# First pair's row maxima in another order, with fills, bias rows and loads moved

## The chip, the cores and the metric

The kernel runs on one core of one Trainium2 chip. The time is device microseconds of a whole execution, and the number compared is the median of several runs. Profiles are of one execution each. The engines are TensorE (PE, its weight loads apart as PEld), VectorE (DVE), ScalarE (ACT), GpSimd (POOL) and SyncE (SP), which here only issues DMAs.

## The reference

Three stages follow one another: attention with queries averaged over pairs of positions, a mixture of 8 experts in which each token goes to one expert, and a dense layer of width 2048 with x * tanh(softplus(x)). The change lies in the attention alone:

```python
q_pool = q.reshape(B, H, S // 2, 2, D).mean(axis=3)      # B 2, H 8, S 1152, D 64
scores = scale * np.matmul(q_pool, k.transpose(0, 1, 3, 2))
scores = scores - np.max(scores, axis=-1, keepdims=True)
attn = np.exp(scores)
attn = attn / (np.sum(attn, axis=-1, keepdims=True) + 1e-09)
attn_out = np.matmul(attn, v)
```

So each of the 576 pooled queries of a head needs the maximum over 1152 keys before its exponentials can be taken.

## The kernel before

The 16 heads are worked on as 8 pairs (p from 0 to 7; h is the head within a pair). A pair has 9 steps (t from 0 to 8), one for each 128 keys. A step makes the scores of its keys for both heads (`scores`, L322 and L324), takes their exponentials on ScalarE into a tile "pt", and every third step multiplies three such tiles by the values (`pv`, L341) and sums them (`psums`, L373). Operands are split in a high part in TensorE's own format (fp32r) and a low rest: `qhi` (tile "qs") and `khi` (tile "at", in halves c of 576 keys) are ScalarE copies, `qlo` (the lower 64 partitions of "qs") and `klo` (tile "Bt") are subtractions on VectorE or GpSimd. `qsum` adds the two positions of each pooled query (tile "tq"), `qcopy` copies the high half of the queries to "qb". Rows 64 and 65 of "Bt" are ones (`bias_rows`), and rows 64 and 65 of "qb" hold the negative maximum and its rounding rest; so the product at L322 adds the low part and subtracts the maximum at once.

The maxima are made before a pair's steps begin, in 9 units: 4 blocks of 128 queries for each head and one shared last unit with the last 64 queries of both heads (`qmix` puts them together in "QM"). A unit has three products of 128x384, called thirds, made by `max_chunk` (L237, and L241 for the shared unit): third 0 takes the first 384 keys and is reduced by VectorE (L103); third 1 takes the difference of the second and the last 384 keys (`kdiff`, tile "kx") and goes through a relu on ScalarE; third 2 takes the last 384 keys, and one fused VectorE operation (L251) adds the relu and takes the maximum. Third 0 of pair 0 uses the three "mx" banks of the PSUM, thirds 1 and 2 of pair 0 the three "sc" banks; for later pairs all use "mx".

`max_cols` then makes columns with the negative maximum and its rest in "Mt" (a reduction, a scaling, and the last operation L97). `max_rows` turns them into rows with TensorE transposes (L295 for queries 0 to 511, L297 for the last 64) and copies the rows into "qb" on ScalarE: 512 and 64 columns for each head. All heads' rows of the first 512 lie in one bank.

For pairs 1 to 7 the units are spread over the steps of earlier pairs (`step_chunks`). For pair 0 there is no earlier step: its 27 thirds are issued ahead of step 0, in the order that `ahead` gives (third 1 of the next unit, third 2 of this one, third 0 of the next), and the other work of this lead stage is put between them by a table, `sched`, filled with `at_step`; steps with p = -1 are the lead. `sched` also gives the order by hand for steps 0 to 8 of pair 0: slot 0 comes right after the scores, slot 1 after the step's first units, slots 4, 2 and 3 behind the value products. Each engine works strictly in the order written; waits follow from the data. `warm` issues junk products of 128x512 on TensorE (L721) whose result nobody reads: 13 at the start, then 9, 7 and 3 around `max_rows`. Tokens (`G.tensor_copy(wait_, ...)`) make GpSimd wait for one element before it goes on.

Buffers that matter: "kd" (raw keys) 3, so that the fourth load, pair 1's second head, waits until `klo` and `khi` of the first keys are done; "pt" 4, shared by raw queries of pairs 0 and 1 and the exponentials; "tq" 3; "kx" 3. All loads named here are issued by SyncE in the order written; the second halves of later queries are added by DMAs that GpSimd issues (`add_q`).

Of the kernel before, what the change touches and what calls it, by code (L numbers as in the profile page):

```python
# [9 lines left out]
F32 = mybir.dt.float32  # L10
# [5 lines left out]
ALU = mybir.AluOpType  # L16
# [4 lines left out]
P = 128  # L21
B, H, S, D = 2, 8, 1152, 64
SQ = S // 2
# [61 lines left out]
def kernel(ctx, tc, cst, qt, kt, v, wgo, w1, w2, wio, out):  # L85
# [4 lines left out]
    def act(out, in_, func=AF.Copy, **kw):  # L90
        A.activation(out=out, in_=in_, func=func, **kw)  # L91

    def tt(eng, out, a, b, op):
        eng.tensor_tensor(out=out, in0=a, in1=b, op=op)  # L94
# [100 lines left out]
    def qlo(p, h):  # L195
        q_ = QS[p, h][64:]
        tt(G if p > 1 or (p, h) == (0, 1) else V, q_, tqt[p, h][64:], q_.bitcast(F32), ALU.subtract)

# [3 lines left out]
    def qb_(p, h):  # L202
        if (p, h) not in QB:
            QB[p, h] = ap.tile([P, SQ], F32R, name="qb", bufs=NBL)
        return QB[p, h]
# [46 lines left out]

    def ahead(units):
        n = len(units)
        seq_ = [(units[0], 0), (units[0], 1)]
        for i in range(n):
            if i + 1 < n:
                seq_ += [(units[i + 1], 1)]
            seq_ += [(units[i], 2)]
            if i + 1 < n:  # L260
                seq_ += [(units[i + 1], 0)]
        return [(*u, c) for u, c in seq_]

    units = [(h, j) for h in range(2) for j in range(4)] + [(0, 4)]
    chunks = ahead(units)
    FIRST = [[0, 1], [2], [3], [4, 5], [6, 7], [8], []]

# [23 lines left out]
    def max_rows(p):  # L291
        mt = Mt[p % 2]
        ps0 = mxp.tile([P, 512], F32, name="mx")
        for j in range(4):
            T.transpose(ps0[:34, j * P:(j + 1) * P], mt[:, j, :], ident)  # L295
        ps1 = mxp.tile([P, 512], F32, name="mx")
        T.transpose(ps1[:34, :P], mt[:, 4, :], ident)  # L297
        for h in range(2):
            act(qb_(p, h)[64:66, :512], ps0[32 * h:32 * h + 2, :])
            act(qb_(p, h)[64:66, 512:], ps1[:2, 64 * h:64 * h + 64])  # L300
# [257 lines left out]
    def at_step(p, t, *fns, slot=0):  # L558
        sched.setdefault((9 * p + t, slot), []).extend(fns)

    at_step(-1, 1, lambda: None, lambda: None, lambda: qhi(0, 1), lambda: (khi(0, 1, 0), qlo(0, 1)))
    at_step(-1, 2, lambda: None, lambda: None, lambda: khi(0, 1, 1), lambda: (klo(0, 0, 0), klo(0, 0, 1)))
    at_step(-1, 3, lambda: qmix(0, 1), lambda: (klo(0, 1, 0), klo(0, 1, 1)))
    at_step(-1, 4, lambda: (qcopy(0, 0), load_k(1, 1), load_q(1, 1)))
    at_step(-1, 5, lambda: qcopy(0, 1))
    at_step(-1, 6, lambda: (qsum(1, 0), khi(1, 0, 0), kdiff(1, 0)))
    at_step(-1, 7, lambda: (qhi(1, 0), khi(1, 0, 1)))
    at_step(-1, 8, lambda: (max_cols(0), qlo(1, 0)))
    at_step(0, 0, lambda: (qmix(1, 0), klo(1, 0, 0), klo(1, 0, 1), kdiff(1, 1), load_q(2, 0), load_k(2, 0)))
    at_step(0, 0, lambda: qsum(1, 1), slot=3)  # L570
    at_step(0, 1, lambda: (qhi(1, 1), khi(1, 1, 0), qlo(1, 1), add_q(2, 0)), slot=1)
    at_step(0, 2, lambda: khi(1, 1, 1))
    at_step(0, 3, lambda: qmix(1, 1), slot=1)
    at_step(0, 2, lambda: (klo(1, 1, 0), klo(1, 1, 1), load_q(2, 1), load_k(2, 1)), slot=1)
    at_step(0, 3, lambda: (qhi(2, 0), kdiff(2, 0), qlo(2, 0), add_q(2, 1)), slot=2)
# [4 lines left out]
    at_step(5, 1, lambda: G.memset(sm[:, :64], 0.0), slot=3)  # L580
    at_step(-1, 8, lambda: load_v(0))
    wait_ = ap.tile([P, 1], F32, name="wait")
# [76 lines left out]
    for i in range(2):  # L659
        G.memset(Mt[i], 0.0)  # L660
        G.memset(Mp[i], 0.0)
    G.memset(one16, 1.0)
    G.memset(zero16, 0.0)
# [9 lines left out]
    def bias_rows(i):  # L673
        act(Bt[i][64:66, :].rearrange("p (a b) -> p a b", b=P), one16[64:66].unsqueeze(1).to_broadcast([2, KT, P]))

    for i in range(2):
        bias_rows(i)
    for i in range(2, NBL):
        at_step(0, i, lambda i=i: bias_rows(i))
    qsum(0, 0)  # L680
# [5 lines left out]
    load_k(1, 0)  # L686
    SP.dma_start(out=wbd, in_=wgo)
    khi(0, 0, 0)
    qlo(0, 0)
    qmix(0, 0)  # L690
    khi(0, 0, 1)
    G.tensor_copy(wait_[64:], QS[0, 0][64:, SQ - 1:].bitcast(F32))
    kdiff(0, 0)
    qsum(0, 1)
# [22 lines left out]
    def warm(n):  # L717

        w = scp.tile([P, 512], F32, name="sc").rearrange("p (a b) -> p a b", b=P)
        for _ in range(n):  # L720
            mm(w, lhsT=one16, rhs=one16.unsqueeze(1).to_broadcast([P, 4, P]), start=True, stop=True)  # L721

    warm(13)
    for g in range(-9, 0):
        tasks = list(sched.get((g, 0), ()))
        for i in range(4):
            if tasks:
                tasks.pop(0)()
            if chunks:
                max_chunk(0, *chunks.pop(0))  # L730
        for f in tasks:
            f()
        if g == -1:
            assert not chunks
            warm(9)
            max_rows(0)
            warm(7)
            for u in FIRST[0]:
                max_chunk(1, *units[u], 1)
            warm(3)  # L740

# [894 lines left out]
```

## Time and profile before

| | |
|---|---|
| median of 3 runs | 651.24 us (649.33 to 652.01) |
| the profiled execution | 648.99 us, its span 647.1 us, mean granted TensorE clock 0.989 |
| PE busy | 618.0 us, 96% of the span |
| DVE busy | 486.1 us, 75% |
| ACT busy | 396.4 us, 61% |
| POOL busy | 254.5 us, 39% |
| chain that ended last | PE 66%, DVE 15%, ACT 7%, issue 5%, DMA 3%, POOL 2% |

The span begins with the first instruction; what lies around it in the execution's time is 1.9 us. Busy shares are means over stages that have different limits; the change touches about the first 35 us, and the rows below are mostly from there. In a timeline a row is one instruction or a run of like ones: its start, its duration, engine, line, operation, tiles and count, and in brackets how long the engine had been idle before it and what released it.

### The profile page before, as it was taken

The numbers are of one execution on the slowest core, as the hardware profiler recorded it, in microseconds if no ns is written. First come the engines' busy times: TensorE is split into PE (matmuls) and PEld (weight loads), VectorE is DVE, ScalarE is ACT, GpSimd is POOL, SyncE is SP. The second block draws the span as 40 slices with busy tenths as digits, with TensorE's granted clock in tenths as the row PEclk, the third lists the DMA queues.
The fourth block names the chain that finished last, engine by engine and source line by source line (L and its number), as shares of the span: only waits on it lengthen the run. The fifth ranks groups of instructions, "written<-read, shape, count | busy, mean of one in ns | idle before, by whom it ended". The sixth has DMA issues, their size and how long they took to land.

```text
span 647.1 us, 11371 instructions
## 1 busy us (share of the span) xinstructions
PE 618.0 (96%) x4144; PEld 496.3 (77%) x4144; DVE 486.1 (75%) x995; ACT 396.4 (61%) x841; POOL 254.5 (39%) x235
## 2 busy tenths in 40 slices
PE   7999999999999999589999999999999999999996
PEld 4667778787787776279868868697879999999993
DVE  4667797978787879558847778249998778878775
ACT  7789888887887675244555367346655545454453
POOL 6747638384664342242215035103223332323221
PEclk8999999999999999699999999999999999999999
DMA  6956655364451332498798496820000200000001
GB/s 248 322 152 207 174 179 125 109 189 147 120 191 34 123 86 66 132 325 305 247 389 316 172 351 238 318 81 0 2 0 1 95 5 1 2 32 18 1 0 52
DMA packets 27405, 89.86 MB, mean 139 GB/s; under 512 B 2886, under 2 KB 7631, under 8 KB 23250
## 3 DMA queue, kind: packets, MB, share of 16 engines
q1 hardware_dynamic: 22176, 74.80, 32.6%
q0 software_dynamic: 3568, 8.79, 5.9%
q10 hardware_dynamic: 1602, 5.51, 2.6%
q8 instruction: 34, 0.56, 0.4%
q14 instruction: 25, 0.20, 0.1%
HBM read 79.65 MB, written 9.97 MB: 138 GB/s over the span
## 4 chain that ended last, share of the span: by engine, by line
PE 66%; DVE 15%; ACT 7%; issue 5%; DMA 3%; POOL 2%; SPq 0%; ACTq 0%; DVEq 0%; POOLq 0%
PE pv L341 10%; PE ops L1454 8%; PE mx L237 5%; PE sc L324 5%; PE sc L322 5%; DVE l L97 4%; DVE n L97 3%; DMA wt<-in_w 3%; PE zps L1023 3%; PE pv L373 3%; PE zps L1024 3%; PE zps L1025 3%; PE yp L1023 3%; PE yp L1025 2%; PE yp L1024 2%
## 5 line engine op out<-in xcount | busy, mean ns | idle before, releaser
L100 POOL TENSOR_SCALAR u<-u 128x384 f32<-128x384 f32 x46 | 58.2, 1265 | 147.0 <-ACT u L91 147.0
L91 ACT ACTIVATE pt<-sc 128x320 f32<-128x320 f32 (+1 forms) x198 | 87.8, 490 | 10.7 <-PE sc L322 7.9
L341 PE MATMUL pv<-pt,vt 128*64 128x288 f32 x576 | 75.6, 411 | 0.0
L91 ACT ACTIVATE l<-n,two 128x384 f32<-128x384 f32 x48 | 29.6, 617 | 74.6 <-DVE n L97 74.6
L103 DVE TENSOR_REDUCE Mp<-mx 128x1 f32<-128x384 f32 x72 | 40.1, 556 | 39.6 <-PE mx L237 34.6
L324 PE MATMUL sc<-qs,at 128*128 128x320 f32 (+1 forms) x264 | 67.4, 299 | 0.0
L322 PE MATMUL sc<-qb,Bt 66*128 66x320 f32 (+1 forms) x264 | 66.6, 296 | 0.0
L1023 PE MATMUL zps<-yh,wh 128*128 128x384 f32 x184 | 63.0, 343 | 1.8 <-DVE n L97 1.8
L1025 PE MATMUL zps<-yl,wh 128*128 128x384 f32 x184 | 61.9, 337 | 0.0
L341 PEld LDWEIGHTS pv<-pt,vt 128*64 128x64 f32 x576 | 39.0, 137 | 28.5 <-issue 5.2
L1024 PE MATMUL zps<-yh,wd 128*128 128x384 f32 x176 | 59.1, 336 | 0.0
L1454 PE MATMUL ops<-wh,gl 128*128 128x512 f32 x144 | 56.9, 400 | 1.4 <-DVE gl L94 0.8
L1454 PE MATMUL ops<-wh,gh 128*128 128x512 f32 x144 | 57.2, 397 | 0.9 <-ACT gh L91 0.9
L1454 PE MATMUL ops<-wd,gh 128*128 128x512 f32 x135 | 53.2, 394 | 0.0
L100 POOL TENSOR_SCALAR dm<-dm 128x512 f32<-128x512 f32 x21 | 41.5, 1977 | 23.1 <-ACT dm L91 23.0
L94 POOL TENSOR_TENSOR Bt<-kd,at 64x576 fp32r<-64x576 f32 x32 | 45.7, 1442 | 4.2 <-ACT at L91 4.1
L324 PEld LDWEIGHTS sc<-qs,at 128*128 128x128 f32 x264 | 46.2, 189 | 1.1 <-issue 0.8
L97 DVE SCALAR_TENSOR_TENSOR l<-n,r 128x384 f32<-128x384 f32 x48 | 26.7, 556 | 25.6 <-ACT r L91 25.6
L322 PEld LDWEIGHTS sc<-qb,Bt 66*128 66x128 f32 x264 | 45.3, 189 | 0.0
L1023 PEld LDWEIGHTS zps<-yh,wh 128*128 128x128 f32 x184 | 34.6, 188 | 4.6 <-DVE n L97 3.1
L237 PE MATMUL mx<-at,qs 128*128 128x384 f32 x120 | 35.7, 363 | 2.3 <-DVE qs L94 0.8
L1053 POOL DMA_INDIRECT ybuf<-y,six x11 | 11.2, 1020 | 66.2 <-ACT y L91 48.4
(327 smaller groups left out, 1615.0 us busy)
## 6 DMA issues: line engine op xcount, KB each, us to landing
wt<-in_w SPq DMA_DIRECT2D x32, 1024.0 KB, 8.0
kd<-in_kt SPq DMA_DIRECT2D x16, 576.0 KB, 5.3
wraw<-in_wio SPq DMA_DIRECT2D x11, 512.0 KB, 4.6
wd<-in_wio SPq DMA_DIRECT2D x11, 512.0 KB, 4.1
vt<-in_v SPq DMA_DIRECT2D x8, 576.0 KB, 5.7
wraw<-in_wio ACTq DMA_DIRECT2D x7, 512.0 KB, 5.8
tq<-in_qt SPq DMA_DIRECT2D x12, 288.0 KB, 4.4
tq<-in_qt POOLq DMA_DIRECT2D x12, 288.0 KB, 6.0
```

What stands on the lines that cost most here:

```text
L91: A.activation(out=out, in_=in_, func=func, **kw)
L94: eng.tensor_tensor(out=out, in0=a, in1=b, op=op)
L97: V.scalar_tensor_tensor(out=out, in0=a, scalar=s, in1=b, op0=op0, op1=op1)
L100: eng.tensor_scalar(out=out, in0=a, scalar1=s1, scalar2=s2, op0=op0, op1=op1)
L237: mm(ps, lhsT=QS[p, h][:, j * P:(j + 1) * P], rhs=keys(h), start=True, stop=True)
L322: mm(o, lhsT=Bt[(2 * p + h) % NBL][:66, ks], rhs=QB[p, h][:66, qs_], start=False, stop=last_, skip_group_check=not (first and last_))
L324: mm(o, lhsT=At[p, h][:, ks], rhs=QS[p, h][:, qs_], start=first, stop=False, skip_group_check=not (first and last_))
L341: mm(pvt[p][f][64 * h:64 * h + 64, :HQ], lhsT=vt[p][:, t, h, :], rhs=Pt[p, t][:, h, f * HQ:(f + 1) * HQ], start=t == 0, stop=t == KT - 1, ...
L1023: mm(out_, lhsT=a, rhs=c, start=first, stop=False)
L1024: mm(out_, lhsT=b_, rhs=c, start=False, stop=False)
L1025: mm(out_, lhsT=a, rhs=d, start=False, stop=last_)
L1454: mm(opt[b_, j], lhsT=(g_, g_, gl_)[i], rhs=(wo, wl_, wo)[i], start=f == 0 and i == 0, stop=f == NF - 1 and i == 2)
```

## The change

`qlo` of pair 0's second head is made in two pieces, queries 0 to 255 and 256 to 575. The order of pair 0's thirds is written out anew (`order0`): third 0 of units 0 and 1 first, then third 1 of both, and from there on third 0 of a unit, its third 1 and third 2 of the unit before it; around units 3 to 5 third 2 comes earlier. The fills of the lead hang on named thirds (`tasks`) instead of `sched`. After each third 2 stands one junk product; further junk products are 4, 2 and 1 instead of 9, 7 and 3, and they write a bank of the value products ("pv0") instead of an "sc" bank. The first `kdiff` goes to VectorE, and GpSimd's token waits for it. Of pair 0's second key halves `klo` moves behind the maxima, into step 0; pair 1's `klo` moves from step 0 to step 2, its second head's to step 3, and GpSimd waits there for the second head's `qlo`, and before step 0's work for the columns "Mt". `qmix` of pair 1's first head moves from step 0 to step 3; `qcopy` of pair 0 and `khi` of pair 1 come behind the last third 1. All four `bias_rows` are made at the start, the last two on VectorE. The raw queries of pair 1's second head and the values of pair 0 are loaded in the first burst; the keys of pair 1's second head are loaded after `max_rows`. For pair 0 `max_rows` transposes the second head's columns once more into a bank of their own, and VectorE copies the row from there.

```diff
--- before.py
+++ after.py
@@ -193,8 +193,9 @@
         act(QS[p, h], tqt[p, h])
 
     def qlo(p, h):
-        q_ = QS[p, h][64:]
-        tt(G if p > 1 or (p, h) == (0, 1) else V, q_, tqt[p, h][64:], q_.bitcast(F32), ALU.subtract)
+        for c in (slice(0, 256), slice(256, SQ)) if (p, h) == (0, 1) else (slice(0, SQ),):
+            q_ = QS[p, h][64:, c]
+            tt(G if p > 1 or (p, h) == (0, 1) else V, q_, tqt[p, h][64:, c], q_.bitcast(F32), ALU.subtract)
 
     def qmix(p, h):
         act(QM[p % 2][:, 192 * h:192 * h + 64], QS[p, h][:, 4 * P:].bitcast(F32))
@@ -250,19 +251,11 @@
             r_ = rlt.pop((p, h, j))
             V.tensor_tensor_reduce(out=r_, in0=ps, in1=r_, scale=1.0, scalar=-3.0e38, op0=ALU.add, op1=ALU.max, accum_out=Mp[p % 2][:, h, j, 1:2])
 
-    def ahead(units):
-        n = len(units)
-        seq_ = [(units[0], 0), (units[0], 1)]
-        for i in range(n):
-            if i + 1 < n:
-                seq_ += [(units[i + 1], 1)]
-            seq_ += [(units[i], 2)]
-            if i + 1 < n:
-                seq_ += [(units[i + 1], 0)]
-        return [(*u, c) for u, c in seq_]
-
     units = [(h, j) for h in range(2) for j in range(4)] + [(0, 4)]
-    chunks = ahead(units)
+    order0 = [(0, 0), (1, 0), (0, 1), (1, 1), (0, 2)]
+    for i in range(2, 9):
+        order0 += [(i, 0), (i, 1)] + [(u, 2) for u in ({3: (2, 3), 4: ()}.get(i, (i - 1,)))]
+    order0 += [(8, 2)]
     FIRST = [[0, 1], [2], [3], [4, 5], [6, 7], [8], []]
 
     def step_chunks(p, t):
@@ -295,8 +288,14 @@
             T.transpose(ps0[:34, j * P:(j + 1) * P], mt[:, j, :], ident)
         ps1 = mxp.tile([P, 512], F32, name="mx")
         T.transpose(ps1[:34, :P], mt[:, 4, :], ident)
+        pa = [(act, ps0[32 * h:32 * h + 2, :]) for h in range(2)]
+        if p == 0:
+            ps2 = mxp.tile([P, 512], F32, name="mx")
+            for j in range(4):
+                T.transpose(ps2[:2, j * P:(j + 1) * P], mt[:, j, 32:34], ident)
+            pa[1] = V.tensor_copy, ps2[:2, :]
         for h in range(2):
-            act(qb_(p, h)[64:66, :512], ps0[32 * h:32 * h + 2, :])
+            pa[h][0](qb_(p, h)[64:66, :512], pa[h][1])
             act(qb_(p, h)[64:66, 512:], ps1[:2, 64 * h:64 * h + 64])
 
     F0 = 256
@@ -558,27 +557,19 @@
     def at_step(p, t, *fns, slot=0):
         sched.setdefault((9 * p + t, slot), []).extend(fns)
 
-    at_step(-1, 1, lambda: None, lambda: None, lambda: qhi(0, 1), lambda: (khi(0, 1, 0), qlo(0, 1)))
-    at_step(-1, 2, lambda: None, lambda: None, lambda: khi(0, 1, 1), lambda: (klo(0, 0, 0), klo(0, 0, 1)))
-    at_step(-1, 3, lambda: qmix(0, 1), lambda: (klo(0, 1, 0), klo(0, 1, 1)))
-    at_step(-1, 4, lambda: (qcopy(0, 0), load_k(1, 1), load_q(1, 1)))
-    at_step(-1, 5, lambda: qcopy(0, 1))
-    at_step(-1, 6, lambda: (qsum(1, 0), khi(1, 0, 0), kdiff(1, 0)))
-    at_step(-1, 7, lambda: (qhi(1, 0), khi(1, 0, 1)))
-    at_step(-1, 8, lambda: (max_cols(0), qlo(1, 0)))
-    at_step(0, 0, lambda: (qmix(1, 0), klo(1, 0, 0), klo(1, 0, 1), kdiff(1, 1), load_q(2, 0), load_k(2, 0)))
+    at_step(0, 0, lambda: (klo(0, 0, 1), klo(0, 1, 1), kdiff(1, 1), load_q(2, 0), load_k(2, 0)))
     at_step(0, 0, lambda: qsum(1, 1), slot=3)
     at_step(0, 1, lambda: (qhi(1, 1), khi(1, 1, 0), qlo(1, 1), add_q(2, 0)), slot=1)
     at_step(0, 2, lambda: khi(1, 1, 1))
-    at_step(0, 3, lambda: qmix(1, 1), slot=1)
-    at_step(0, 2, lambda: (klo(1, 1, 0), klo(1, 1, 1), load_q(2, 1), load_k(2, 1)), slot=1)
+    at_step(0, 3, lambda: (qmix(1, 0), qmix(1, 1)), slot=1)
+    at_step(0, 2, lambda: (G.tensor_copy(wait_[64:], QS[1, 1][64:, :1].bitcast(F32)), klo(1, 0, 0), klo(1, 0, 1), load_q(2, 1)), slot=1)
+    at_step(0, 3, lambda: (klo(1, 1, 0), klo(1, 1, 1), load_k(2, 1)), slot=1)
     at_step(0, 3, lambda: (qhi(2, 0), kdiff(2, 0), qlo(2, 0), add_q(2, 1)), slot=2)
     at_step(0, 4, lambda: (qcopy(1, 0), qcopy(1, 1), load_q(3, 0), load_q(3, 1)), slot=1)
     at_step(0, 6, lambda: (khi(2, 0, 0), khi(2, 0, 1), qhi(2, 1), add_q(3, 0), add_q(3, 1)), slot=1)
     at_step(0, 6, lambda: (after(2, 0), qlo(2, 1), kdiff(2, 1)), slot=3)
     at_step(0, 8, lambda: (G.tensor_copy(tri, cc("tri")), G.tensor_copy(iota16, iota), G.tensor_copy(code16, cc("code")), G.tensor_copy(tid16, cc("tid"))), slot=1)
     at_step(5, 1, lambda: G.memset(sm[:, :64], 0.0), slot=3)
-    at_step(-1, 8, lambda: load_v(0))
     wait_ = ap.tile([P, 1], F32, name="wait")
 
     def after(n, u):
@@ -659,7 +650,7 @@
     for i in range(2):
         G.memset(Mt[i], 0.0)
         G.memset(Mp[i], 0.0)
-    G.memset(one16, 1.0)
+    V.memset(one16, 1.0)
     G.memset(zero16, 0.0)
     G.memset(xu4, 0.0)
     G.memset(sm, 0.0)
@@ -671,12 +662,11 @@
         G.memset(e2[:, h, h:h + 1], 1.0)
 
     def bias_rows(i):
-        act(Bt[i][64:66, :].rearrange("p (a b) -> p a b", b=P), one16[64:66].unsqueeze(1).to_broadcast([2, KT, P]))
-
-    for i in range(2):
+        cp_ = act if i < 2 else V.tensor_copy
+        cp_(Bt[i][64:66, :].rearrange("p (a b) -> p a b", b=P), one16[64:66].unsqueeze(1).to_broadcast([2, KT, P]))
+
+    for i in range(NBL):
         bias_rows(i)
-    for i in range(2, NBL):
-        at_step(0, i, lambda i=i: bias_rows(i))
     qsum(0, 0)
     qhi(0, 0)
     load_q(0, 1)
@@ -685,12 +675,13 @@
     load_q(1, 0)
     load_k(1, 0)
     SP.dma_start(out=wbd, in_=wgo)
+    load_q(1, 1)
+    load_v(0)
     khi(0, 0, 0)
     qlo(0, 0)
-    qmix(0, 0)
     khi(0, 0, 1)
-    G.tensor_copy(wait_[64:], QS[0, 0][64:, SQ - 1:].bitcast(F32))
-    kdiff(0, 0)
+    kdiff(0, 0, V)
+    G.tensor_copy(wait_, KD[0, 0][:, :1].bitcast(F32))
     qsum(0, 1)
     kdiff(0, 1)
 
@@ -716,28 +707,35 @@
 
     def warm(n):
 
-        w = scp.tile([P, 512], F32, name="sc").rearrange("p (a b) -> p a b", b=P)
+        w = pvp.tile([P, 512], F32, name="pv0").rearrange("p (a b) -> p a b", b=P)
         for _ in range(n):
             mm(w, lhsT=one16, rhs=one16.unsqueeze(1).to_broadcast([P, 4, P]), start=True, stop=True)
 
     warm(13)
-    for g in range(-9, 0):
-        tasks = list(sched.get((g, 0), ()))
-        for i in range(4):
-            if tasks:
-                tasks.pop(0)()
-            if chunks:
-                max_chunk(0, *chunks.pop(0))
-        for f in tasks:
-            f()
-        if g == -1:
-            assert not chunks
-            warm(9)
-            max_rows(0)
-            warm(7)
-            for u in FIRST[0]:
-                max_chunk(1, *units[u], 1)
-            warm(3)
+    tasks = {
+        (1, 1): lambda: (qhi(0, 1), qlo(0, 1), klo(0, 0, 0)),
+        (2, 1): lambda: (khi(0, 1, 0), klo(0, 1, 0), qsum(1, 0), kdiff(1, 0)),
+        (3, 1): lambda: khi(0, 1, 1),
+        (4, 1): lambda: qmix(0, 0),
+        (5, 1): lambda: (qmix(0, 1), khi(1, 0, 0)),
+        (8, 1): lambda: (qhi(1, 0), qcopy(0, 0), qcopy(0, 1), khi(1, 0, 1)),
+    }
+    for i, c in order0:
+        max_chunk(0, *units[i], c)
+        if (i, c) in tasks:
+            tasks[i, c]()
+        if c == 2:
+            warm(1)
+    warm(4)
+    max_cols(0)
+    qlo(1, 0)
+    G.tensor_copy(wait_, Mt[0][:, 0, 1:2])
+    max_rows(0)
+    load_k(1, 1)
+    warm(2)
+    for u in FIRST[0]:
+        max_chunk(1, *units[u], 1)
+    warm(1)
 
     def run(g, slot):
         for f in sched.get((g, slot), ()):
```

## Rows read from the trace of the kernel before

**Rows 1.** Busy time by stage: stretch, each engine's busy us (instructions), PEclk, DMA share, GB/s.

```profile
7.00:23.27 16.27, 13.82 (x57) 8.41 (x57) 10.53 (x31) 11.44 (x26) 15.26 (x13) 0.90 0.73 280
23.27:34.01 10.74, 9.06 (x50) 7.04 (x49) 6.95 (x18) 9.20 (x21) 6.56 (x6) 1.00 0.79 257
...
60.00:100.00 40.00, 39.84 (x341) 30.93 (x340) 33.02 (x75) 33.65 (x79) 22.48 (x22) 1.00 0.56 168
```

**Rows 2.** Timeline, VectorE, 4 to 20 us; the last row is from 44.86.

```profile
4.59 0.76 DVE L94 TENSOR_TENSOR tq<-pt 128x576 f32<-128x576 f32 x1 [4.59 <-DMA pt<-in_qt]
...
7.52 0.56 DVE L103 TENSOR_REDUCE Mp<-mx 128x1 f32<-128x384 f32 x1 [0.67 <-PE mx L237]
...
9.71 0.56 DVE L251 CUSTOM_DVE_ANT_0 wd<-sc,wd 128x384 f32<-128x384 f32 x1 [1.63 <-PE sc L237]
...
10.66 0.55 DVE L251 CUSTOM_DVE_ANT_0 wd<-sc,wd 128x384 f32<-128x384 f32 x1
...
13.56 0.56 DVE L251 CUSTOM_DVE_ANT_0 wd<-sc,wd 128x384 f32<-128x384 f32 x1 [0.93 <-PE sc L237]
...
18.75 0.08 DVE L251 DVE_READ_ACCUMULATOR2_ANT Mp<- 128x1 f32 x1
...
19.28 0.61 DVE L97 SCALAR_TENSOR_TENSOR Mt<-mfin,Mt 128x10 f32<-128x10 f32 x1
...
44.86 0.18 DVE L97 SCALAR_TENSOR_TENSOR Mt<-mfin,Mt 128x10 f32<-128x10 f32 x1
```

**Rows 3.** Timeline, GpSimd, 7 to 20 us.

```profile
7.01 0.18 POOL L692 COPY wait<-qs 64x1 f32<-64x1 f32 x1 [4.09 <-DVE qs L94]
...
7.28 0.99 POOL L94 TENSOR_TENSOR kx<-kd 128x384 fp32r<-128x384 f32 x1
...
8.23 1.42 POOL L94 TENSOR_TENSOR tq<-pt 128x576 f32<-128x576 f32 x1
...
12.93 4.20 POOL L94 TENSOR_TENSOR Bt<-kd,at 64x576 fp32r<-64x576 f32 x3
...
18.44 1.41 POOL L94 TENSOR_TENSOR tq<-pt 128x576 f32<-128x576 f32 x1
```

**Rows 4.** Timeline, ScalarE and TensorE, 19 to 24 us.

```profile
19.89 0.68 ACT L91 ACTIVATE qs<-tq 128x576 fp32r<-128x576 f32 x1 [2.11 <-POOL tq L94]
...
19.94 0.61 PE L295 MATMUL mx<-cs,Mt 128*34 128x128 f32 x4
...
20.50 1.67 PE L721 MATMUL sc<-one 128*128 128x512 f16 x7
...
21.16 1.52 ACT L91 ACTIVATE qb<-mx 2x512 fp32r<-2x512 f32 x4
...
22.50 0.45 PE L237 MATMUL mx<-kx,qs 128*128 128x384 f32 x1 [0.15 <-ACT qb L91]
...
23.27 0.50 PE L324 MATMUL sc<-qs,at 128*128 128x320 f32 x1
```

**Rows 5.** Timeline, ScalarE and TensorE, 28 to 35 us.

```profile
28.73 0.68 ACT L91 ACTIVATE at<-kd 128x576 fp32r<-128x576 f32 x1
...
31.53 1.16 ACT L91 ACTIVATE Bt<-one 2x1152 fp32r<-2x1152 f16 x1
...
32.70 1.37 PE L237 MATMUL mx<-at,qs 128*128 128x384 f32 x3 [0.74 <-ACT Bt L91]
...
34.01 3.13 PE L341 MATMUL pv<-pt,vt 128*64 128x288 f32 x24
```

**Rows 6.** TensorE by half microseconds: stretch, busy (count), PEclk, DMA share, GB/s.

```profile
8.50:9.00 0.50, 0.50 (x2) 0.50 1.00 403
```

**Rows 7.** Timeline, TensorE, the same stretch.

```profile
9.36 0.52 PE L237 MATMUL mx<-at,qs 128*128 128x384 f32 x1
9.68 0.52 PE L237 MATMUL sc<-kx,qs 128*128 128x384 f32 x1
```

**Rows 8.** The raw key tiles' loads up to 40 us, issue to landing.

```profile
DMA to landing us min/median/max: 3.9/5.9/9.4
```

## The prediction

> **What bounds the kernel now.** I read the busy time by stage first, then each engine's timeline up to 35 us, then the granted clock there, and last how long the key loads took to land. The first view says where a change can pay [rows 1]. From 60 us on TensorE is busy 39.84 of 40 us: nothing in this diff touches that part, so an earlier start should move it as a block. Before that TensorE is not the limit. Between 7.00 and 23.27 us, where the row maxima of the first pair are made, it is busy 13.82 of 16.27 us, junk products included; from 23.27 to 34.01, the first three score steps and the beginning of the fourth, 9.06 of 10.74 us, while ScalarE has 9.20. The diff works in these two stretches alone.
>
> In the first, VectorE sets the pace [rows 2]. It makes one unit (a reduction and a fused add-and-maximum) in 0.95 us (the fused operations start at 9.71 and 10.66), and two waits break the run: 1.63 us ahead of the first fused operation and 0.93 us ahead of the one at 13.56. Both end with a product that waited for GpSimd: the first needs the key difference (made 7.28 to 8.27), the second the low half of the second head's queries, after which GpSimd goes on at 12.93 [rows 3]. The last maximum is done at 18.83, the bias columns at 19.89. From there a second chain runs [rows 4]: ScalarE waits 2.11 us for the sum of pair 1's queries, which GpSimd starts at 18.44 [rows 3] behind four key-low products; then two fills, four copies of bias rows at 21.16, the product at 22.50 that waits for the copies' bank, three junk products, and the first score at 23.27. In the second stretch the place to look at is 31.53 [rows 5]: a 1.16 us fill of bias rows of ones stands in ScalarE's queue ahead of the copies that free TensorE's banks, and TensorE waits 0.74 us at that point for it.
>
> **The change part by part.**
>
> *Lead, VectorE.* The first key difference goes from GpSimd to VectorE, behind the low half of the first queries, for which GpSimd's token at 7.01 waited [rows 3], so from about 6.9. The trace has no VectorE difference of 128x384; it is bounded by the 128x576 one, 0.76, and by 384/576 of that, 0.51 [rows 2]. I take 0.55, near the reduction of the same width, 0.56. It ends at 7.45, before the first reduction can start (7.52, set by the first product), so it costs nothing and the difference is there 0.8 us earlier than the 8.27 of before. The relu of the first second-third can then end by about 8.45, just when VectorE has made the two reductions now put first (7.52 to 8.46). The wait of 1.63 goes.
>
> *Lead, GpSimd.* It now starts after VectorE's difference. Before, the operation behind its token began at 7.28, 0.27 after the token and some 0.4 after what this waited for [rows 3], so the sum of the second head's queries starts at 7.85 instead of 8.23. Its 1.42 us and 0.99 for the second key difference bring it to 10.25, and the low half of the queries in two pieces follows: unsplit 1.40, as the three in 4.20; two pieces cannot cost less than that nor more than two 128x384 differences, 1.98. I take 1.6, the first ending at 11.0. VectorE wants its first product at 7.52 + 8 x 0.47 = 11.3. So this wait goes as well, if a product waits only for its own piece; if it waits for both (11.85) it costs 0.55. Next late is ScalarE: with two fills of 0.6 between the relus of units 2 and 3 I count 0.5 us of waiting for VectorE. The maxima end at 7.52 + 9 x 0.95 + 0.5 = 16.6 (before 18.83).
>
> *Bias columns.* Their last operation took 0.61 us at 19.28, and 0.18 us for pair 1 at 44.86 [rows 2]; the difference is that at 19.28 GpSimd was in a 1.41 us sum until 19.85 [rows 3]. Now GpSimd should be past its pair-1 difference (17.0) and waits for the columns: 0.17 + 0.17 + 0.18 and gaps, 0.65 in all, hence 17.3 instead of 19.89. The Trainium skill (SBUF — State Buffer, the section that states the single rule of the shared port pair) says that a VectorE operation with two SBUF inputs and a GpSimd one that reads SBUF exclude each other for whole instructions; the two durations agree. By that rule the low half of pair 1's queries on VectorE, which now starts together with GpSimd's next key-low product, could also be the loser and end 1.4 us later, at about 19.5; the score start would slip some 0.4 us and the total would be 647.1.
>
> *The chain that ends last.* GpSimd now makes two key-low products instead of four before the pair-1 sum: 10.25 + 1.6 + 2 x 1.4 = 14.65, and 1.41 more: 16.05 (before 19.85). Behind it ScalarE has four fills (high half, two query copies, second key half), at 0.635 each as the two between 19.89 and 21.16 [rows 4]: 18.6. The columns at 17.3 plus five transposes (0.61 for four) are ready before, so this chain decides, 2.56 us earlier than 21.16. The row copies: four took 1.52; the second head's 512 columns go to VectorE, from a bank of their own. That copy is between 0.38 (a quarter of the four) and 512/384 of a reduction, 0.75; I take 0.7, and it runs beside ScalarE's remaining three: by columns 0.68 of the 1.52 would go, but each copy has a fixed part, so I take off 0.57 and leave 0.95. The four added transposes cost TensorE between 0 and 0.61, while it waits anyway. The product that waited until 22.50 can start at 18.6 + 0.95 = 19.55, 2.95 earlier. After it stands one junk product instead of three, 0.24 each (1.67 for seven); of the 0.48 I count 0.4. First score: 23.27 - 2.95 - 0.4 = 19.9. **Term 1: 3.35 us**; it would be 2.0 if the transposes and the VectorE copy were on the path in full, and 3.9 if GpSimd's chain closed up so far that the columns decided.
>
> *Steps 0 to 3.* The fill at 31.53 moves to VectorE and to the beginning. There VectorE is idle until 4.59 [rows 2]; two such copies of 1152 columns cost between 0.36 (two operations of 0.18) and 4 x 0.76 = 3.04 (each as two additions of 576 columns); I take 2.3, as ScalarE's 1.16 each. They start near 1 us, so even the dearest are covered; without the cover a late one would delay the first sum, and with it all, one for one. ScalarE's next copies can start 1.16 us earlier, and TensorE's products at 32.70 and the value products at 34.01 follow [rows 5]. **Term 2: 1.15 us**, bounded below by the 0.74 that TensorE showed and above by 1.4 with the small query fill that also leaves step 0. The other such fill, a step later, I count as nothing, since TensorE is in the value products then.
>
> *Moved at no cost.* Pair 1's key-low products go to steps 2 and 3 on GpSimd, which is idle 4.2 of the 10.74 us there [rows 1]; their readers come nine steps later. Fewer junk products: TensorE was waiting. The two early loads stand at the end of SyncE's queue, behind all that the lead needs; queued in front of nothing but the late key load.
>
> Sum: 4.5 us. The profiled execution, 648.99, would become 644.5. It lies 2.25 under the median, so I set the forecast against the median: 651.24 - 4.5 = **646.7 us**.
>
> **Rivals.**
>
> *The clock (slower).* TensorE's granted clock was 0.50, the 1.2 GHz level, at 8.5 [rows 6], after it had idled between the junk and the first products and again until the key difference; there the products start 0.32 us apart [rows 7]. A unit with its new junk product would take 3 x 0.32 + 0.43 = 1.39 us at that level (0.43 is 512/384 of 0.32), against VectorE's 0.95. If the low level held through the whole lead, nine units would end at 7.0 + 12.5 + 0.5 = 20.0, the columns at 20.7 and the first score at about 23.3: nothing won; and if it held on through half of the score steps, TensorE's 9.06 us of work there would grow by 4.5, of which 1.7 is idle now: about +3, **654 us**. The decision lies where the low level lasts past about 14 us. For it: the gap ahead of the first product stays, and each later wait has fewer junk products in it. Against it: the second of the two gaps goes, and work plus junk is denser. The Trainium skill (TensorE: Matmul & The Clock Gate, What's actually happening) calls the low level the default that activity lifts, which would make the removal of junk the thing to watch; the trace's fall after the idle stretch agrees.
>
> *The late key load.* The load of pair 1's second keys went out within the lead before; now it waits for a key-low product that itself waits for the columns: 17.3, 0.4 for the token and 1.4, so issue at about 19.1. ScalarE reaches its first use (28.73 before [rows 5]) at 28.73 - 3.35 = 25.4. Six key loads took 3.9, 5.9 (median) and 9.4 us to land [rows 8]: at 4.5, which I expect with no queue ahead of it, there is 1.8 us to spare; at the longest ScalarE stands for 3.1 us with the exponentials behind the fill. Gain then 4.5 - 3.1 = 1.4: **649.8 us**. It decides from a landing above 6.3 us.
>
> *The lead gives half.* A product waits for both pieces, relus stand behind fills more often than I counted, and the port collision comes as the rule has it: some 0.5 each, and the ScalarE chain a little later: gain 2.2 to 2.8, **648.8 us**. For it: ScalarE is at 11.44 of 16.27 us now and gets more between the relus.
>
> *The change does not do what it says* is covered by these: if the first maxima do not start earlier, the GpSimd chain still does.
>
> **How the numbers follow.** Forecast 0.60 (its own range 645 to 648), lead half 0.16, late load 0.12, clock 0.08, better than the forecast (the score steps give more, as the waits of 23 to 34 us add to 1.7) 0.04. A change under 0.5%, 3.26 us, is about what a measurement of this kernel can tell from none: three runs spread over 2.7 us. Faster by more than that: 0.04 better and 0.56 of the forecast's 0.60, 0.60. Within: the forecast's remaining 0.04, 0.16 and 0.12, 0.32. Slower: 0.08. The range leaves out most of the clock case and the tails: 643.5 (the upper bounds of both terms, 5.3, and 2.4 for runs on the low side) to 650.5 (the late load, and 0.7 for runs on the high side).
>
> **What would show it.** In the changed kernel's timeline: first fused operation near 8.5 and no wait over 0.6 us in VectorE's nine units; last maximum near 16.6; pair 1's sum on GpSimd near 14.65; the first row copy near 18.6 and the first score near 19.9; value products of step 3 near 29.4; everything after 60 us shifted by 4 to 5 us. Wrong would be: a first score after 21, a key fill in step 1 that waits for a DMA, a granted clock of 0.50 after 14 us, or a shift that shrinks between 35 and 60 us.

## The result and the profile after

The changed kernel takes 644.99 us (median of 6 runs, 644.41 to 646.71) against 650.3 for the kernel before in the same comparison: a ratio of 0.9919 with a 95% interval of 0.9900 to 0.9938, 5.3 us less where 4.5 were forecast. Run again beside three experiments it gave 0.9953 (0.9935 to 0.9971), 644.33 against 647.79: 3.5 us less by the medians, 3.0 by the ratio. Both intervals exclude a ratio of 1. The two estimates lie on both sides of the forecast, and why they differ is open; their intervals overlap only at their edges, 0.9935 to 0.9938.

Stage by stage, the stretches that answer to [rows 1] (from 7 us to the first score, from there to the first value products), with the columns of that group:

```profile
7.00:19.65 12.65, 12.17 (x57) 7.30 (x58) 11.33 (x33) 9.98 (x24) 11.45 (x12) 1.00 0.64 260
19.65:29.39 9.74, 8.95 (x51) 7.07 (x50) 6.63 (x18) 8.51 (x21) 7.02 (x7) 1.00 0.84 277
```

16.27 us became 12.65, and 10.74 became 9.74. The granted clock is 1.00 in both, where [rows 1] had 0.90 in the first. VectorE's timeline against [rows 2]:

```profile
8.51 0.56 DVE L252 CUSTOM_DVE_ANT_0 wd<-sc,wd 128x384 f32<-128x384 f32 x1
...
16.69 0.08 DVE L252 DVE_READ_ACCUMULATOR2_ANT Mp<- 128x1 f32 x1
...
17.22 0.17 DVE L97 SCALAR_TENSOR_TENSOR Mt<-mfin,Mt 128x10 f32<-128x10 f32 x1
```

No wait stands ahead of the first fused operation (the bracket is missing); the maxima end at 16.77 and the columns at 17.39, their last operation at 0.17 us. GpSimd against [rows 3], with the two pieces of the low half and the late keys' first use:

```profile
7.76 1.41 POOL L94 TENSOR_TENSOR tq<-pt 128x576 f32<-128x576 f32 x1
...
10.21 1.57 POOL L94 TENSOR_TENSOR qs<-tq,qs 64x256 fp32r<-64x256 f32 x2
...
14.61 1.42 POOL L94 TENSOR_TENSOR tq<-pt 128x576 f32<-128x576 f32 x1
...
23.43 1.50 POOL L94 TENSOR_TENSOR kx<-kd 128x384 fp32r<-128x384 f32 x1 [2.46 <-DMA kd<-in_kt]
```

And ScalarE and TensorE against [rows 4] and [rows 5]:

```profile
10.99 0.44 PE L238 MATMUL mx<-at,qs 128*128 128x384 f32 x1
...
16.06 0.68 ACT L91 ACTIVATE qs<-tq 128x576 fp32r<-128x576 f32 x1 [0.23 <-POOL tq L94]
...
17.79 0.67 ACT L91 ACTIVATE at<-kd 128x576 fp32r<-128x576 f32 x1
18.48 0.79 ACT L91 ACTIVATE qb<-mx 2x512 fp32r<-2x512 f32 x3
18.65 0.68 DVE L298 CAST qb<-mx 2x512 fp32r<-2x512 f32 x1 [0.47 <-PE mx L295]
...
19.17 0.60 PE L238 MATMUL mx<-kx,qs 128*128 128x384 f32 x2
...
19.65 0.50 PE L323 MATMUL sc<-qs,at 128*128 128x320 f32 x1
...
25.13 0.68 ACT L91 ACTIVATE at<-kd 128x576 fp32r<-128x576 f32 x1
```

The first score comes at 19.65 instead of 23.27, the value products of step 3 at 29.39 instead of 34.01: 4.62 us won at the end of the stretch that the change touches. At the token counts behind the attention (their first product at 265.5 before, 260.7 after) the shift is 4.8. In the second profile of the changed kernel the same three marks stand at 20.14, 29.90 and 261.3, which makes 4.1 and 4.2 us for the last two. The two profiled spans differ by only 3.1 (647.1 and 644.0): this execution of the changed kernel lost 1.5 us between 327 and 420 us, in the expert stage, which the change does not touch. TensorE's waits there, for this execution and for the second profile of the same kernel (whose span is 642.1); columns are who waited for whom, total us, times, longest. This execution comes first:

```profile
PE hps L1022 <- DVE w1l L94: 2.2, 2, 1.6
PE hps L1021 <- DVE hl L97: 1.4, 1, 1.4
```

```profile
PE hps L1022 <- DVE w1l L94: 1.0, 2, 0.6
PE hps L1021 <- DVE hl L97: 0.5, 1, 0.5
```

So that loss belongs to one execution. The stretch up to 30 us is the place to read the experiments by.

### The profile page after: what moved, and what is told of

It reads as the page before. It is cut to its first block, busy times and chain, and to the rows that moved or that the text cites. A ratio compares the mean times of both kernels' runs of the same rounds, so it can differ in the third digit from the quotient of the medians.

```text
span 644.0 us, 11380 instructions
## 1 busy us (share of the span) xinstructions
PE 615.7 (96%) x4145; PEld 494.9 (77%) x4145; DVE 490.6 (76%) x1000; ACT 393.2 (61%) x838; POOL 255.9 (40%) x236
## 4 chain that ended last, share of the span: by engine, by line
PE 67%; DVE 16%; ACT 7%; issue 5%; DMA 3%; POOL 1%; SPq 0%; ACTq 0%; DVEq 0%
PE pv L340 10%; PE ops L1452 8%; PE mx L238 5%; PE sc L321 5%; PE sc L323 5%; DVE l L97 4%; DVE n L97 3%; PE zps L1021 3%; DMA wt<-in_w 3%; PE pv L372 3%; PE zps L1022 3%; PE zps L1023 3%; PE yp L1021 3%; PE yp L1023 3%; PE yp L1022 2%
## 5 line engine op out<-in xcount | busy, mean ns | idle before, releaser
L1051 POOL DMA_INDIRECT ybuf<-y,six x11 | 11.3, 1027 | 66.4 <-ACT y L91 48.3
```

## The experiments

The totals of single parts differ by about as much as one comparison resolves, so each run is read by marks in its profile. In 10 of the 11 profiles that have the first difference on VectorE, GpSimd's sum of the second head's queries starts later than 7.76, because it waits 0.33 to 1.00 us for its load. The second profile of the changed kernel shows it:

```profile
8.15 1.42 POOL L94 TENSOR_TENSOR tq<-pt 128x576 f32<-128x576 f32 x1 [0.64 <-DMA pt<-in_qt]
```

Therefore the table counts from the start of that sum: to the end of the bias columns, to the first score, and from the first score to the value products of step 3. The ratio is to the kernel before of the same comparison. Each row of marks is from one profile. Two chains are told apart below: the columns (VectorE's maxima, then the bias columns) and the fill chain (GpSimd up to pair 1's query sum, then four ScalarE fills). Both end at the row copies, ahead of two products for pair 1 and the first score.

| run | ratio (95%) | sum starts | columns | first score | score to value products |
|---|---|---|---|---|---|
| before | 1 | 8.23 | +11.66 | +15.04 | 10.74 |
| changed | 0.9919 (0.9900 to 0.9938) | 7.76 | +9.63 | +11.89 | 9.74 |
| changed_again | 0.9953 (0.9935 to 0.9971) | 8.15 | +9.75 | +11.99 | 9.76 |
| klo_back | 1.0029 (1.0009 to 1.0049) | 7.93 | +9.76 | +14.66 | 11.92 |
| old_order | 0.9959 (0.9943 to 0.9975) | 7.99 | +10.27 | +12.14 | 9.75 |
| bias_back | 0.9963 (0.9948 to 0.9978) | 7.98 | +9.74 | +11.93 | 10.78 |
| one_bank | 0.9956 (0.9933 to 0.9979) | 8.34 | +9.82 | +12.43 | 10.16 |
| no_unit_junk | 0.9948 (0.9930 to 0.9967) | 8.31 | +10.59 | +12.47 | 9.73 |
| junk_9_7_3 | 0.9986 (0.9970 to 1.0001) | 8.27 | +9.75 | +13.97 | 9.73 |
| no_token | 0.9971 (0.9956 to 0.9986) | 8.47 | +10.71 | +13.27 | 9.76 |
| kdiff_back | 0.9944 (0.9925 to 0.9963) | 8.14 | +10.12 | +12.00 | 9.74 |
| free_banks | 0.9933 (0.9906 to 0.9960) | 8.48 | +9.75 | +11.16 | 9.88 |
| free_banks_fills | 0.9933 (0.9912 to 0.9954) | 8.57 | +9.73 | +11.13 | 9.60 |
| before_junk_gap | 1.0000 (0.9985 to 1.0014) | 7.94 | +11.23 | +14.61 | 10.78 |

**Key-low products back (klo_back).**

```diff
-        (2, 1): lambda: (khi(0, 1, 0), klo(0, 1, 0), qsum(1, 0), kdiff(1, 0)),
-        (3, 1): lambda: khi(0, 1, 1),
+        (2, 1): lambda: (khi(0, 1, 0), klo(0, 1, 0)),
+        (3, 1): lambda: (khi(0, 1, 1), klo(0, 1, 1), qsum(1, 0), kdiff(1, 0)),
...                                # klo(0, 0, 1) behind klo(0, 0, 0); both gone from step 0
```

> The changed kernel with the two key-low products of the second key halves put back ahead of the pair-1 sum on GpSimd. Theory (the chain GpSimd sum, four ScalarE fills, row copies decides the first score): the sum starts at 17.4 instead of 14.61, the first score comes at about 22.4 instead of 19.65, and the time is 647.8 us against 645.0. Rival (VectorE's maxima decide, the GpSimd chain has slack): the columns are done at 17.39 as before, the first score stays at 19.7, the time at 645.0.

The columns are no later, the pair-1 sum starts at 17.57, and the first score follows by 14.66 instead of 11.9 to 12.0: the theory's 2.8. The time grew by far more, to slower than before. TensorE had been idle for 2.77 us ahead of the two products at 22.11, and the granted clock fell as the scores began (in the rows of stretches: length, TensorE's busy us and its instructions, the granted clock, DMA share, GB/s):

```profile
22.11 0.60 PE L238 MATMUL mx<-kx,qs 128*128 128x384 f32 x2 [2.77 <-ACT qb L91]
```

```profile
22.00:23.00 1.00, 0.90 (x5) 1.00 0.95 352
23.00:24.00 1.00, 1.00 (x7) 0.59 1.00 405
24.00:26.00 2.00, 1.99 (x7) 0.50 1.04 227
```

It stayed at 0.50, the 1.2 GHz level, until 30, and the way to the value products took 11.92 us instead of 9.75: 2.2 us on top. That the clock is the cause of all 2.2 is read from these rows; no run holds the clock up there.

**The old order of thirds (old_order).**

```diff
-    order0 = [(0, 0), (1, 0), (0, 1), (1, 1), (0, 2)]
-    for i in range(2, 9):
-        order0 += [(i, 0), (i, 1)] + [(u, 2) for u in ({3: (2, 3), 4: ()}.get(i, (i - 1,)))]
-    order0 += [(8, 2)]
+    order0 = [(0, 0), (0, 1)]
+    for i in range(9):
+        order0 += [(i + 1, 1)] * (i < 8) + [(i, 2)] + [(i + 1, 0)] * (i < 8)
```

> The changed kernel with the thirds of pair 0 in the order of the kernel before (one unit ahead), all else as changed. Theory (the fill chain decides): VectorE waits about 0.5 us for the first relu and the columns come up to 0.5 us later than 17.39, but they have about 0.4 us to spare, so the first score stays within 0.2 us of 19.65 and the time at 645.0 to 645.2. Rival (the maxima's order is what brought the gain): columns 1 to 2 us later, first score at 20.6 to 21.6, time 646 to 647.

Counted from the sum, the columns come 0.5 to 0.6 us later and the first score 0.15 to 0.25 later: the theory, at the edge of its 0.2. Here the row copies wait for the transposes, so the columns end last:

```profile
18.96 0.79 ACT L91 ACTIVATE qb<-mx 2x512 fp32r<-2x512 f32 x3 [0.22 <-PE mx L287]
```

The ratio's interval overlaps with that of the changed kernel's second comparison and lies above that of its first.

**Fills of ones back on ScalarE (bias_back).**

```diff
-        cp_ = act if i < 2 else V.tensor_copy
+        cp_ = act                       # i = 2, 3 again in steps 2 and 3
```

> The changed kernel with the two later fills of ones back on ScalarE behind the scores of steps 2 and 3. Theory (term 2 of the prediction): first score unchanged at 19.65, value products of step 3 at 30.5 instead of 29.39, time 646.1 us. Rival (hidden once the start is earlier): value products within 0.3 us of 29.4, time 645.0.

First score unchanged at +11.93 (at 19.91, with the sum 0.2 us later), 10.78 us from there to the value products, as before the change (10.74): 1.0 us, term 2. The row that did it, and its end:

```profile
28.21 1.16 ACT L91 ACTIVATE Bt<-one 2x1152 fp32r<-2x1152 f16 x1
29.39 0.87 ACT L91 ACTIVATE wd<-mx 128x384 f32<-128x384 f32 x2
```

**Rows from one bank (one_bank).**

```diff
-        if p == 0:
+        if False:
             ps2 = mxp.tile([P, 512], F32, name="mx")
```

> The changed kernel with the second head's rows copied by ScalarE from the bank of the first head's rows, without the four added transposes. Theory: ScalarE has four copies in a row again (1.5 us from 18.1 or 18.5 on) and the product behind them waits 0.5 us longer; first score at 20.1 to 20.2, time 645.5. Rival (the copies are covered by junk and transposes): first score within 0.1 us of 19.65.

First score 0.45 to 0.55 later, as expected. The stretch behind it is 0.4 longer as well, which was not expected: the sum of pair 1's second queries on VectorE took 1.40 us instead of 0.75, and in the new alignment GpSimd's key difference had started before it. A product behind it waits 0.44 us for VectorE, where that of the changed kernel's second profile waits 0.32 for ScalarE. VectorE, GpSimd and TensorE of that run:

```profile
24.43 1.40 DVE L94 TENSOR_TENSOR tq<-pt 128x576 f32<-128x576 f32 x1
```

```profile
24.20 1.01 POOL L94 TENSOR_TENSOR kx<-kd 128x384 fp32r<-128x384 f32 x1 [2.48 <-PE mx L238]
```

```profile
27.70 0.94 PE L238 MATMUL mx<-kx,qs 128*128 128x384 f32 x2 [0.44 <-DVE qs L94]
```

**The changed kernel again (changed_again).**

> The changed kernel itself once more, beside the three kernels run with it and on the same chip. Any theory: first score at 19.6 to 19.7, value products of step 3 at 29.4, no fall of the granted clock before 250 us, time about 5 us under the kernel before.

First score at 20.14, half a microsecond later than expected, all of it the load that the sum waits for and the small rest from sum to score; the steps after it are the same to 0.02 us. The time is 3.5 us under the kernel before instead of about 5. So the 7.76 of the first profile, without a wait, was a lucky execution.

**No junk between units (no_unit_junk).**

```diff
-        if c == 2:
-            warm(1)
```

> The changed kernel without the nine junk products between the units. Theory (the products of the maxima themselves, now without the two gaps, keep the clock up): granted clock 1.00 from 7 to 25 us, first score at 19.5 to 19.7, time as the changed kernel's. Rival (the junk keeps it up): the clock falls to 0.50 somewhere from 8 to 25 us; if within the maxima, columns up to 1 us later; if at the first scores, as in the run with the key-low products put back, value products of step 3 at 31 to 32 and the time 2 us longer.

The rival's first branch. TensorE was busy 0.63, 0.41 and 0.70 of the microseconds from 9, 10 and 11 on, and the clock fell at about 12.6 (reckoned from the 0.79):

```profile
9.00:10.00 1.00, 0.63 (x4) 1.00 1.01 413
10.00:11.00 1.00, 0.41 (x2) 1.00 1.03 424
11.00:12.00 1.00, 0.70 (x3) 1.00 1.01 399
12.00:13.00 1.00, 1.00 (x6) 0.79 1.04 414
13.00:14.00 1.00, 1.00 (x5) 0.50 1.05 428
```

The columns came 0.85 to 0.95 later, the first score 0.5 to 0.6, and the steps behind it were undisturbed. The time cannot be told from that of the changed kernel beside it.

**9, 7 and 3 junk products (junk_9_7_3).**

```diff
-    warm(4)
+    warm(9)    # likewise 2 -> 7 and 1 -> 3
```

> The changed kernel with 9, 7 and 3 junk products around the rows, as in the kernel before, instead of 4, 2 and 1. Theory (junk stands in TensorE's order ahead of the first score): the two products for pair 1 start at about 19.9 instead of 19.17, the first score at 20.6 to 20.8, value products of step 3 at 30.4, time 1.1 us longer. Rival (TensorE waits for ScalarE's row copies anyway, as the prediction had it for all but 0.4 us): first score at 20.0 to 20.1.

First score 2.0 us later counted from the sum, more than either expected:

```profile
16.54 2.55 PE L712 MATMUL pv<-one 128*128 128x512 f16 x10
18.92 0.60 PE L288 MATMUL mx<-cs,Mt 128*34 128x128 f32 x4
19.36 0.27 PE L290 MATMUL mx<-cs,Mt 128*34 128x128 f32 x1
19.47 0.60 PE L295 MATMUL mx<-cs,Mt 128*2 128x128 f32 x4
19.90 1.67 PE L712 MATMUL pv<-one 128*128 128x512 f16 x7
21.23 0.70 PE L238 MATMUL mx<-kx,qs 128*128 128x384 f32 x2
```

The columns were done at 18.02, but the transposes started at 18.92, behind the first batch; the second batch then stood ahead of the two products. The ratio, 0.9986, gives most of the gain back.

**No token for the columns (no_token).**

```diff
-    G.tensor_copy(wait_, Mt[0][:, 0, 1:2])
```

> The changed kernel without GpSimd's token that waits for the bias columns. Theory (VectorE's operation with two SBUF inputs waits out a whole GpSimd operation, as at 19.28 in the kernel before): the key-low product starts at 17.0 and the columns' last operation ends with it at about 18.4 instead of 17.39; first score at 20.4 to 20.7, time 0.8 to 1.0 us longer. Rival (no such exclusion, 0.61 before had another cause): that operation takes 0.18, first score unchanged at 19.65.

The theory, and it happened twice: the columns' last operation took 1.15 us, and the low half of pair 1's queries behind it 1.91 instead of 0.76, while GpSimd was in two key-low products from 17.75 on. VectorE, then GpSimd:

```profile
18.03 1.15 DVE L97 SCALAR_TENSOR_TENSOR Mt<-mfin,Mt 128x10 f32<-128x10 f32 x1
19.21 1.91 DVE L94 TENSOR_TENSOR qs<-tq,qs 64x576 fp32r<-64x576 f32 x1
```

```profile
17.75 2.76 POOL L94 TENSOR_TENSOR Bt<-kd,at 64x576 fp32r<-64x576 f32 x2
```

First score 1.3 to 1.4 us later, more than the 0.8 to 1.0 expected for one such wait. The first of the two ends with GpSimd's first product (about 19.15), the second 0.6 us after GpSimd's last (20.51), a little less than the 0.76 of its own work.

**First difference on GpSimd (kdiff_back).**

```diff
-    kdiff(0, 0, V)
-    G.tensor_copy(wait_, KD[0, 0][:, :1].bitcast(F32))
+    G.tensor_copy(wait_[64:], QS[0, 0][64:, SQ - 1:].bitcast(F32))
+    kdiff(0, 0)
```

> The changed kernel with the first key difference back on GpSimd, behind a token for the low half of the first queries. Theory (the chain from the second head's query sum on GpSimd decides; in most executions that sum waits for its load until 8.0 to 8.5): VectorE's first fused operation comes at about 9.2 instead of 8.5, the sum starts at 8.2 to 8.4, and the first score follows the sum by 11.9 to 12.2 us as in the changed kernel (11.9 and 12.0). Rival (VectorE's wait, back again, decides): 12.6 us or more from the sum to the first score.

The theory: first fused operation at 9.25, sum at 8.14, columns 0.4 to 0.5 later than in the changed kernel, first score at +12.00, as there. The score follows the columns by 1.88 here, so their spare time is used up.

**Free banks, and free banks with other fills (free_banks, free_banks_fills).**

```diff
+        ps0 = pvp.tile([P, 512], F32, name="pv1") if p == 0 else mxp.tile([P, 512], F32, name="mx")
+        ps1 = pvp.tile([P, 512], F32, name="pv0") if p == 0 else mxp.tile([P, 512], F32, name="mx")
-    warm(2)
-    warm(1)
```

```diff
+        (2, 1): lambda: (khi(0, 1, 0), qsum(1, 0), klo(0, 1, 0), kdiff(1, 0)),   # the second run, besides
+        (7, 1): lambda: qhi(1, 0),                                              # khi(1, 0, 1) behind max_rows
```

> The changed kernel with the transposes of pair 0's columns written to the two banks of the value products, which are free until step 3, and without the last three junk products. Theory (the two products for pair 1 wait only for a bank that ScalarE's row copies hold): they start when the low half of pair 1's queries is there, at about 10.8 us behind the second head's query sum instead of 11.4, and the first score 11.3 to 11.6 us behind it instead of 11.9 to 12.0; time 0.3 to 0.6 us shorter, within what can be measured. Rival (the first score waits for the rows themselves): 11.8 to 12.0.

> As the run with the free banks, and pair 1's query sum ahead of one key-low product on GpSimd, its high half right behind the relu of unit 7, and the second key half of pair 1 behind the row copies on ScalarE. Theory (the fill chain and the columns then end together): row copies start as soon as the transposes are done, 10.3 us behind the second head's query sum instead of 10.7, first score 11.0 to 11.3 us behind it; time 0.6 to 0.9 us under the changed kernel. Rival (the fill that now stands behind the row copies delays relus and exponentials as much): first score 11.0 to 11.3, but value products of step 3 more than 10.2 us after it instead of 9.75.

The free banks, together with three junk products fewer, bring the first score to +11.16, 0.7 to 0.8 earlier than in the changed kernel and a little under the 11.3 to 11.6 expected; which of the two did it was not run apart. The other fills add nothing to that: the row copies wait 1.13 us for the transposes there, so the columns decide. But the value products come another 0.3 earlier (+20.73 from the sum, against +21.04 and, in the changed kernel, +21.63 and +21.75). Both ratios, 0.9933, lie between those of the changed kernel: in the total neither can be told from it.

**The kernel before with its gap filled (before_junk_gap).**

```diff
+                if g == -9 and i == 0:
+                    warm(5, pvp, "pv0")    # warm takes the bank as arguments
```

> The kernel before with five more junk products behind its first product, in the gap until the key difference is there. Theory (VectorE and GpSimd set the pace of the old lead, so the fall of the clock cost nothing there): granted clock 1.00 from 7 to 25 us, or at least no fall at 8.5; first score within 0.2 us of 23.27 and the time that of the kernel before. Rival (part of the gain was the clock): first score 0.5 to 1.5 us earlier than 23.27.

No fall of the clock, and the first score at 22.55, 0.72 earlier than 23.27, which is the rival's range. But 0.29 of it is there when the sum starts (the first queries' sum on VectorE starts at 4.29 instead of 4.59, with its load); from the sum the score comes 0.43 earlier (+14.61 against +15.04), between the two. The time is unchanged, 1.0000 (0.9985 to 1.0014).

## Why the prediction was right

**The chain.** In the first profile most steps landed within 0.3 us: first fused operation 8.51 (forecast near 8.5), query sum 7.76 (7.85), the two pieces 1.57 (1.6), pair-1 sum 14.61 (14.65), columns 17.39 (17.3), first row copy 18.48 (18.6), first score 19.65 (19.9), value products 29.39 (29.4). A product does wait only for its own piece: the one at 10.99 starts while the second piece runs until 11.78. Term 1 measured 3.62 us (forecast 3.35), term 2 1.00 (1.15). The 0.27 by which term 1 came out larger is mostly the sum that started 0.09 earlier, without a wait, and the way from the first row copy to the first score, 1.17 us where 1.3 was counted. The first of these is luck. The absolute forecast, 646.7, was set against a median of 651.24; the kernel before came out at 650.3 in the comparison itself, so 0.9 of the 1.7 us between 646.7 and 644.99 is the reference and not the change.

**What decides.** The claim that the fill chain ends last was shown by klo_back (fills late, columns not: score late by the whole amount), and kdiff_back agrees (columns 0.4 to 0.5 late, score not). In the changed kernel's own profile the row copies at 18.48 follow the last fill (17.79) without a wait. The chain that the profile itself follows back from the first score is the other one, through junk, transposes and columns, since the junk products' modelled end (19.04) covers the wait; only the experiment tells the two apart. The runs give its margin too. In old_order and no_unit_junk the score follows the columns by 1.87 and 1.88; in the changed kernel the columns would allow it at 9.75 + 1.87 = +11.6, and the fills hold it to +11.9 to +12.0. So the columns have 0.3 to 0.4 to spare, and undoing the first difference's move, the new order or the unit junk costs the first score only 0.0 to 0.1, 0.15 to 0.25 and 0.5 to 0.6: part of what each delays is hidden by the other chain. The parts do not add up: the losses at the first score from undoing one part each (klo_back, junk_9_7_3, no_token, one_bank, no_unit_junk, old_order) come to some 7 us, twice term 1.

**Where it was mis-sized.** "Fewer junk products: TensorE was waiting", with 0.4 us for the last two, was right for the old schedule and not for the new one: there the old junk costs 2.0 us, because the waits that covered it are gone. The prediction gave the cover for the old schedule, but not the price in the new one. The step that put the query sum at 7.85 left out its load: GpSimd did not wait for it in the first profile of the changed kernel, and waited 0.33 to 1.00 us in ten others. It is the new wait at the head of the chain; with sums starting at 7.93 to 8.57 there, between a fifth and all of the 0.38 us counted against 8.23 is given back (all of it in six of the ten).

**The rivals.** The clock (slower) did not come: 1.00 throughout the lead, in both profiles. That the clock can fall here is shown: without the unit junk it fell in the lead, and the columns came 0.9 us later; with TensorE idle 2.77 us ahead of the scores it fell there, and 2.2 us were lost. The fall in the kernel before cost about 0.4 us, an estimate from one pair of profiles (before and before_junk_gap). The late key load had 1.7 us to spare: GpSimd gets it at 23.43, ScalarE needs it at 25.13; forecast 1.8. Two errors cancel in that: it was issued at 19.61 instead of 19.1, and landed within 3.8 us instead of 4.5. By the same reading the other runs that load it behind the maxima have 0.7 us or more (free_banks_fills the least), and in none does ScalarE wait for it. Half a gain in the lead did not come. The collision on the port did not cost VectorE anything: with the token VectorE started first and took 0.76, and GpSimd's token copy took 0.77 instead of 0.18; no_token shows what the token saves, 1.3 us.

```profile
17.43 0.76 DVE L94 TENSOR_TENSOR qs<-tq,qs 64x576 fp32r<-64x576 f32 x1
```

```profile
17.46 0.77 POOL L732 COPY wait<-Mt 128x1 f32<-128x1 f32 x1 [0.48 <-DVE Mt L97]
```

The Trainium skill (SBUF — State Buffer, SBUF: two separate sides) says that of a VectorE operation with two SBUF inputs and a GpSimd one that reads SBUF, the one that starts first holds the shared port pair for its whole instruction; both orders agree with it here.

**What stays open.** Why one comparison gave 5.3 us and the other 3.5. The marks up to 30 us differ by 0.5 between the two profiles of the changed kernel, which is the load; there is no profile of the kernel before beside the second. The ten runs made from the changed kernel speak for the smaller number: if what each loses or wins up to the value products, counted from the sum, is put back, their ratios come to 0.994 to 0.996, an estimate of 3 to 4 us for the whole change. So the 5.3 us rather are the high end, and the 4.5 of the forecast may be some 1 us too much in the total.

Not tried is whether the two loads added to the first burst are what makes the second queries land late. In the two profiles of kernels without them the sum starts at 8.23 and 7.94 behind GpSimd's key difference and shows no wait, which does not decide it. Nor were the split of `qlo`, the moved loads and the moved `qcopy`, `qmix` and pair-1 `klo` undone one by one.

## What to carry to other kernels

When a lead stage has two chains that end within half a microsecond of one another, undoing one part at a time shows which ends last and with how much to spare; do not add the parts up. A filler that is free under a wait has a price as soon as the wait goes: cost it in the new schedule, and count it against what it does for the clock. Read small parts by marks in the trace, counted from the event that starts the chain; the total cannot separate them.

## What the runs showed of the hardware

- A VectorE operation with two SBUF inputs stretched when it started while GpSimd ran on SBUF data: from 0.17 to 1.15 and from 0.76 to 1.91 us (no_token), from 0.75 to 1.40 us (one_bank). A 10-column operation can so cost as much as a 576-column one.
- The landing of one load in the first burst wandered: in the changed kernel and its variants the reader of the second query load started between 7.76 (without a wait) and 8.57 us, behind the same first loads, while the reader of the first query load started at 4.3 to 4.6.
- The granted clock fell as the scores began, after TensorE had idled 2.77 us (klo_back), and it fell in the midst of work, after three microseconds with 0.63, 0.41 and 0.70 of busy time (no_unit_junk). It stayed at 1.00 throughout the lead in all eleven profiles with a junk product for each unit. But it also stayed there in before_junk_gap, without unit junk, while TensorE idled 1.50 us ahead of a product at 12.20; what decides it is not shown.
